# A planner that orders the instructions counts DMA loads as landing later, and four more weight buffers open once the weight conversion is over

## The chip, the cores and the metric

One core of one Trainium2 chip. The time is device microseconds (us) of one execution, taken from several runs; the profile is of one execution. Engines are named as in the profile: PE (TensorE matmul), PEld (TensorE weight load), DVE (VectorE), ACT (ScalarE), POOL (GpSimd), SP (SyncE, which here only issues DMAs; its queue is in order).

## The reference

Three layers follow one another on 4 batches of 448 tokens, 12 heads of 64:

```python
q_n, k_n = rmsnorm(q, g_q), rmsnorm(k, g_k)
scores = q_n @ k_n.T / sqrt(64); attn = softmax(scores)      # max subtracted, 1e-9 in the sum
x = (attn @ v), heads put side by side                       # 1792 x 768
x = max(x @ w_in, 0) ** 2 @ w_out                            # 768 -> 2048 -> 768
h = x @ w_in2; out = (max(h, 0) + alpha * min(h, 0)) @ w_out2
```

The inputs are float32. In the kernel the weights arrive as 64-bit words and are turned into float32 on the chip.

## The kernel before

**Arithmetic.** Each product of the two MLPs is made of three matmuls: every operand is split into a high part (`wh`) and a rest (`wl`), and high x rest, high x high and rest x high are added in PSUM. The weights are cut into units: 32 of the up projection (384 KB each, three 128-row blocks) and 24 of the down projection (512 KB, four blocks). A unit feeds 9 or 12 matmuls for one batch (`T = 1`), or 18 or 24 for two (`T = 2`).

**Three sources of a unit** (`weight`, L265). "first": the 64-bit words are loaded into a `raw` buffer (L282), ACT takes the absolute value of the high words into `ws` (L292), DVE does four steps on it (L294, L297, L301, L304), ACT copies the high part into a `whl` buffer (L251), POOL writes the rest (L259), and the finished pair is stored to DRAM (`w<-whl`, L311). "kept": the finished pair is loaded back from DRAM straight into a `whl` buffer (L279). "f64": like "first", without the store. There are three buffers each of `raw`, `ws` and `whl`, for the whole program.

**Stages.** `with_attention` (L422) holds the attention of all four batches, the first MLP of batch 0 (slot 0, units 0 to 55, source "first") and the first MLP of batch 1 (slot 1, units 56 to 111, source "kept"). The row maxima of the scores (L685 on PE, L689 on DVE) travel through PE and ACT into a small DMA (`mv<-mn`, L697) before the scores proper (L710) can start. `without` (L826) follows: the first MLP for batches 2 and 3 (units 112 to 167, "kept"), then the second MLP twice (units 168 to 279, "f64"), all with `T = 2`. The last lines of `with_attention` fetch units 112 to 114 ahead (L821 to L823).

**What sets the order.** The program is written out by a planner (`Tasks`, L53). Every step is a task with an urgency, the engines that may do it and a cost in us. The planner keeps a clock for each engine, always takes the task that can start first (of those within 0.05 us the one with the lower urgency number), and emits it. Every engine, and SP's queue with it, runs in the order of emission, so the costs decide only the order; the waits on the chip are real semaphores. A DMA of cost c that is issued at s is taken to land like this (L159 to L162):

```python
self.ends[e] = s + 0.06
self.dma = max(self.dma, s + 1.3) + t.on[e]
t.end = self.dma + 0.8
```

where the cost is the bytes over 350e3 (L210). By that account a 384 KB unit lands 3.22 us after its issue on an empty queue, a 512 KB unit after 3.60 us. Where several buffers of a pool are free, a task takes the one that came free first (`slot`, L179). MLP matmuls have the largest urgency numbers: PE does them when no attention step can start.

Of the kernel before, what the change touches and what calls it, by code (L numbers as in the profile page):

```python
# [26 lines left out]
UP, DN = 384, 512  # L27
# [25 lines left out]
class Tasks:  # L53
# [45 lines left out]
    def run(self):  # L99
        ready = {e: [] for e in self.ends}  # L100

        def offer(t):
            for e in t.on:
                ready[e].append(t)

        for t in self.new:
            for d in (*t.deps, *t.behind):
                if d.start is None:
                    t.missing += 1
                    d.next.append(t)  # L110
        for t in self.new:
            if not t.missing:
                offer(t)
        left = len(self.new)
        self.new = []
        while left:
            best = None
            for e, tasks in ready.items():
                found, soonest = [], None
                for t in tasks:  # L120
                    s = self.ends[e] + (max(t.gap, self.gap[e]) if e in "AV" else 0)
                    s = max(s, self.port) if e in t.alone else s
                    for d in t.deps:
                        s = max(s, d.end + (0 if d.engine == e == "T" else self.WAIT[e]))
                    for d in t.behind:
                        s = max(s, d.start)
                    taken = []
                    for b in t.bufs:
                        if b.ap is None:
                            taken.append(self.slot(b, taken))  # L130
                            s = max(s, taken[-1][0] + self.WAIT[e]) if taken[-1] else None
                            if s is None:
                                break
                    if s is None:
                        continue
                    if len(t.on) > 1:
                        other = min(max(self.ends[o], s, self.port if o in t.alone else 0) + self.PRICE[o] * t.on[o]
                                    + 0.7 * sum(x.on[o] for x in ready[o] if x.urgency < t.urgency)
                                    for o in t.on if o != e)
                        if s + self.PRICE[e] * t.on[e] > other + 0.2:  # L140
                            continue
                    found.append((s, t.urgency, t))
                    soonest = s if soonest is None else min(soonest, s)
                if found:
                    s, _, t = min((x for x in found if x[0] <= soonest + 0.05), key=lambda x: x[1])
                    if best is None or s < best[0]:
                        best = (s, e, t)
            assert best, "no task can start"
            s, e, t = best
            for o in t.on:  # L150
                ready[o].remove(t)
            for b in t.bufs:
                if b.ap is None:
                    _, n, b.pool = self.slot(b)
                    slots = self.free[b.pool]
                    b.slot = slots.pop(next(i for i, x in enumerate(slots) if x[1] == n))
                    b.ap = b.slot[2]
            t.engine, t.start = e, s
            if e == "S" and t.on[e]:  # L159
                self.ends[e] = s + 0.06  # L160
                self.dma = max(self.dma, s + 1.3) + t.on[e]
                t.end = self.dma + 0.8  # L162
            else:
                t.end = self.ends[e] = s + t.on[e]
                self.gap[e] = t.gap
                if e in t.alone:
                    self.port = t.end
            t.emit(e)
            left -= 1
            for b in t.bufs:  # L170
                b.left -= 1
                b.until = max(b.until, t.end)
                self.release(b)
            for n in t.next:
                n.missing -= 1
                if not n.missing:
                    offer(n)
# [29 lines left out]


def load(nbytes):
    return nbytes / 350e3  # L210


MM = 0.202
# [3 lines left out]
def attention_relu2_mlp_prelu_mlp(ctx: ExitStack, tc: tile.TileContext, qkt, qk_tm, v, gb, alpha, ident, sel,  # L217
# [10 lines left out]
    def pooled(pool, name, n, shape, dtype):  # L228
        ts.pool(name, [pool.tile(shape, dtype, name=f"{name}{i}") for i in range(n)])
# [6 lines left out]
    kept = {id(w1): [Buf(dram.tile([128, 2, UP], F32, name=f"w1_{i}")) for i in range(2 * KF)],  # L236
            id(w2): [Buf(dram.tile([128, 2, DN], F32, name=f"w2_{i}")) for i in range(4 * KD)]}
    y_dram = [[Buf(dram.tile([128, S], F32, name=f"y{b}_{d}")) for d in range(KD)] for b in range(2)]
    for name, n, dt, size in (("raw", 3, U32, 2 * DN), ("ws", 3, F32, DN), ("whl", 3, F32R, 2 * DN)):
        pooled(const, name, n, [128, size], dt)  # L240

    only = {}

# [21 lines left out]
    def weight(u, w, i, source, urgency, after):  # L265

        n = w.shape[-1] // 2
        both = Buf(pool="whl")
        parts = [(both, 0), (both, 1)]

        def part(k):
            return both.ap[:, k * n:k * n + n]

        def pair():
            return both.ap[:, :2 * n].bitcast(F32).rearrange("p (k n) -> p k n", k=2)

        if source == "kept":
            k = kept[id(w)][i]
            add(urgency, {"S": load(1024 * n)}, dma(pair, lambda: k.ap), [k], parts, "wh")  # L279
            return both  # L280
        raw, f = Buf(pool="raw"), Buf(pool="ws")
        add(urgency, {"S": load(1024 * n)}, dma(lambda: raw.ap[:, :2 * n], lambda: w[i]), [], [raw], "raw", after)  # L282

        def half(k):
            return raw.ap[:, :2 * n].rearrange("p (n two) -> p n two", two=2)[:, :, k]

        def fu():
            return f.ap[:, :n].bitcast(U32)


        add(urgency, {"A": act(n)},
            lambda e: nc.scalar.activation(out=f.ap[:, :n], in_=half(1).bitcast(F32), func=ACTF.Abs), [raw], [f], "f")  # L292
        add(urgency, {"V": dve2(n)},
            lambda e: nc.vector.tensor_scalar(out=f.ap[:, :n], in0=f.ap[:, :n], scalar1=TINY, scalar2=None, op0=ALU.max),  # L294
            [], [f])
        add(urgency, {"V": dve2(n)},
            lambda e: nc.vector.tensor_scalar(out=fu(), in0=fu(), scalar1=0x07FFFFFF, scalar2=3,  # L297
                                              op0=ALU.bitwise_and, op1=ALU.logical_shift_left), [], [f])

        add(urgency, {"V": dve(n)},  # L300
            lambda e: nc.vector.scalar_tensor_tensor(out=fu(), in0=half(1), scalar=0xC0000000, in1=fu(),  # L301
                                                     op0=ALU.bitwise_and, op1=ALU.bitwise_or), [raw], [f])
        add(urgency, {"V": dve(n)},
            lambda e: nc.vector.scalar_tensor_tensor(out=fu(), in0=half(0), scalar=29, in1=fu(),  # L304
                                                     op0=ALU.logical_shift_right, op1=ALU.bitwise_or), [raw], [f])
        add(urgency, on("wh", A=act(n), V=dve2(n)), lambda e: copy(e, part(0), f.ap[:, :n]), [f], [(both, 0)], "wh")
        add(urgency, on("wl", P=pool2(n), V=dve(n)), lambda e: rest(e, part(1), f.ap[:, :n], part(0)),
            [f, (both, 0)], [(both, 1)], "wl")
        if source == "first":
            k = kept[id(w)][i]  # L310
            add(urgency, {"S": load(1024 * n)}, dma(lambda: k.ap, pair), parts, [k], "keep")  # L311
        return both

    stream = []
    for s1, more in (("first", 0), ("kept", 0), ("kept", 2)):
        stream += [(w1, i, s1) for i in range(2 * KF)] + [(w2, i, s1) for i in range(4 * KD)]
        for _ in range(more):
            stream += [(w3, i, "f64") for i in range(2 * KF)] + [(w4, i, "f64") for i in range(4 * KD)]
    made, cur = {}, [0]

    def prepare(u, urgency, after=None):
        if u < len(stream) and u not in made:
# [99 lines left out]
    def with_attention():  # L422
        with ExitStack() as es:
# [378 lines left out]
            def give(bank):  # L802
# [3 lines left out]
                    ts.free["m"].append((bank.slot[0], bank.slot[1], bank.ap.rearrange("p (t n) -> p t n", t=1)))  # L806
                add(-100, {"S": 0}, emit, [], [bank], None, first_scores[0, H - 1])

            setup()
            attention(0, 0, True)  # L810
            for _ in range(2):
# [2 lines left out]
                prepare(u, 95, first_scores[0, 7])  # L814
            only.update(wl="P", wh="A")
            mlp(0, (0,), hg, to_dram(1, [y_dram[0]]), 10000, 140, 2.6)
            attention(1, 200)
            mlp(0, (1,), hg, to_dram(1, [y_dram[1]]), 20000, 340, 5.2)
            attention(2, 400)
            attention(3, 600)  # L820
            for u in range(cur[0], cur[0] + 3):  # L821
                prepare(u, 5000)
                made[u].open = True  # L823
            ts.run()

    def without():  # L826
        with ExitStack() as es:
            q1 = es.enter_context(tc.tile_pool(name="q1", bufs=1))
            pp = es.enter_context(tc.tile_pool(name="pp2", bufs=1, space=PSUM))
            hg = fixed(q1, [128, 2, KF, 2, S], F32R, "hg2")  # L830
            pooled(q1, "rl", 3, [128, 2, S], F32)
            pooled(q1, "y", 2, [128, 2, S], F32)
            pooled(pp, "m", 4, [128, 2, 512], F32)
# [83 lines left out]
```

## Time and profile before

| what | value |
|---|---|
| median of 3 runs | 1296.36 us (1292.48 to 1309.52) |
| profiled execution | 1297.45 us, its span 1295.6 us |
| PE busy | 1232.6 us (95%), 5790 matmuls |
| DVE, ACT, POOL busy | 800.8 (62%), 720.9 (56%), 373.5 us (29%) |
| mean granted TensorE clock | 0.978 of full |
| DMA | 194.45 MB, mean 150 GB/s |

The span is from the first to the last instruction; the 1.85 us around it are launch and end. Shares over the whole span mix two very different parts: `with_attention` ends and `without` begins at 590.9 us, and the profile has to be read on either side of that.

### The profile page before, as it was taken

The numbers are of one execution on the slowest core, as the hardware profiler recorded it, in microseconds if no ns is written. First come the engines' busy times: TensorE is split into PE (matmuls) and PEld (weight loads), VectorE is DVE, ScalarE is ACT, GpSimd is POOL, SyncE is SP. The second block draws the span as 40 slices with busy tenths as digits, with TensorE's granted clock in tenths as the row PEclk, the third lists the DMA queues.
The fourth block names the chain that finished last, engine by engine and source line by source line (L and its number), as shares of the span: only waits on it lengthen the run. The fifth ranks groups of instructions, "written<-read, shape, count | busy, mean of one in ns | idle before, by whom it ended". The sixth has DMA issues, their size and how long they took to land.

```text
span 1295.6 us, 16918 instructions
## 1 busy us (share of the span) xinstructions
PE 1232.6 (95%) x5790; PEld 1073.4 (83%) x5790; DVE 800.8 (62%) x1419; ACT 720.9 (56%) x1350; POOL 373.5 (29%) x354
## 2 busy tenths in 40 slices
PE   4997899797999899999999999999999999999998
PEld 2556677675888788888999999999999999999997
DVE  6688899999888688602111000487895548786550
ACT  4788689776699879823333000366653336664331
POOL 3245345535345525310000000222232222223221
PEclk7998999998999899999999999999999999999999
DMA  5136658788445544257333323233354333334330
GB/s 184 54 117 228 237 202 277 275 280 274 170 145 180 193 145 136 81 188 246 105 105 120 114 100 112 83 105 111 125 180 155 119 114 98 114 123 137 133 112 29
DMA packets 69014, 194.45 MB, mean 150 GB/s; under 512 B 8320, under 2 KB 14592, under 8 KB 68928
## 3 DMA queue, kind: packets, MB, share of 16 engines
q1 hardware_dynamic: 68928, 193.38, 45.1%
q8 instruction: 45, 0.74, 0.2%
q14 instruction: 41, 0.34, 0.1%
HBM read 159.84 MB, written 33.42 MB: 149 GB/s over the span
## 4 chain that ended last, share of the span: by engine, by line
PE 80%; DVE 10%; ACT 4%; DMA 3%; issue 2%; SPq 0%; POOL 0%; ACTq 0%; DVEq 0%
PE m L343 54%; PE bank L343 11%; PE bank L710 5%; PE pv L753 4%; PE pv L729 3%; PE bank L685 2%; DVE mc L689 1%; DVE ws L301 1%; DMA whl<-w 1%; DVE hl L259 1%; DVE ws L304 1%; DVE ws L294 1%; DMA tm<-in_qk_tm 1%; DMA raw<-in_w 1%; DVE ss L588 1%
## 5 line engine op out<-in xcount | busy, mean ns | idle before, releaser
L259 POOL TENSOR_TENSOR whl<-ws,whl 128x384 fp32r<-128x384 f32 (+2 forms) x169 | 204.9, 1215 | 683.4 <-ACT whl L251 405.2
L343 PE MATMUL m<-xs,whl 128*128 128x448 f32 x1728 | 350.8, 365 | 0.7 <-ACT rl L251 0.7
L343 PE MATMUL m<-hg,whl 128*128 128x448 f32 x1728 | 350.7, 365 | 0.0
L343 PEld LDWEIGHTS m<-xs,whl 128*128 128x128 f32 x1728 | 324.5, 188 | 26.7 <-ACT rl L251 1.1
L343 PEld LDWEIGHTS m<-hg,whl 128*128 128x128 f32 x1728 | 324.5, 188 | 25.7
L292 ACT ACTIVATE ws<-raw 128x384 f32<-128x384 f32 (+1 forms) x168 | 101.3, 603 | 133.5 <-POOL whl L259 112.3
L294 DVE TENSOR_SCALAR ws<-ws 128x384 f32<-128x384 f32 (+1 forms) x168 | 68.0, 409 | 142.6 <-ACT ws L292 142.4
L343 PE MATMUL bank<-xs,whl 128*128 128x448 f32 x576 | 142.4, 382 | 7.8 <-POOL xs L259 3.3
L251 ACT ACTIVATE whl<-ws 128x384 fp32r<-128x384 f32 (+1 forms) x167 | 94.4, 566 | 77.3 <-PE m L343 57.1
L343 PE MATMUL bank<-hg,whl 128*128 128x448 f32 x576 | 130.6, 369 | 2.2 <-DMA whl<-w 2.2
L343 PEld LDWEIGHTS bank<-xs,whl 128*128 128x128 f32 x576 | 111.5, 196 | 21.2 <-POOL xs L259 3.7
L343 PEld LDWEIGHTS bank<-hg,whl 128*128 128x128 f32 x576 | 108.9, 191 | 11.8 <-DMA whl<-w 2.6
L304 DVE SCALAR_TENSOR_TENSOR ws<-raw,ws 128x384 uint32<-128x384 uint32 (+1 forms) x168 | 116.3, 698 | 2.7
L689 DVE TENSOR_REDUCE mc<-bank 112x1 f32<-112x448 f32 x192 | 110.3, 615 | 11.4 <-PE bank L685 10.2
L259 DVE TENSOR_TENSOR hg<-m,hg 128x896 fp32r<-128x896 f32 x48 | 52.1, 1086 | 94.1 <-ACT hg L251 93.6
L301 DVE SCALAR_TENSOR_TENSOR ws<-raw,ws 128x384 uint32<-128x384 uint32 (+1 forms) x168 | 106.5, 639 | 3.7
L710 PE MATMUL bank<-mv,st 128*128 128x448 f32 (+2 forms) x352 | 102.2, 397 | 5.3 <-ACT mn L695 2.4
L259 DVE TENSOR_TENSOR hl<-bank,hl 128x448 fp32r<-128x448 f32 (+1 forms) x120 | 73.7, 618 | 32.6 <-ACT bank L718 31.5
L753 PE MATMUL pv<-hl,vhl 128*128 128x448 f32 x330 | 87.3, 374 | 1.3 <-DVE hl L259 1.3
L685 PE MATMUL bank<-st,mv 128*112 128x448 f32 x176 | 62.2, 411 | 22.5 <-DVE mc L689 7.8
L710 PEld LDWEIGHTS bank<-mv,st 128*128 128x128 f32 (+2 forms) x352 | 60.9, 182 | 24.9 <-DVE mc L689 6.3
L297 DVE TENSOR_SCALAR ws<-ws 128x384 uint32<-128x384 uint32 (+1 forms) x168 | 72.7, 439 | 3.6
(110 smaller groups left out, 1259.5 us busy)
## 6 DMA issues: line engine op xcount, KB each, us to landing
raw<-in_w SPq DMA_DIRECT2D x96, 384.0 KB
raw<-in_w SPq DMA_DIRECT2D x72, 512.0 KB
whl<-w SPq DMA_DIRECT2D x64, 384.0 KB
whl<-w SPq DMA_DIRECT2D x48, 512.0 KB
w<-whl SPq DMA_DIRECT2D x32, 384.0 KB
w<-whl SPq DMA_DIRECT2D x24, 512.0 KB
qk<-in_qkt SPq DMA_DIRECT2D x24, 448.0 KB
tm<-in_qk_tm SPq DMA_DIRECT2D x40, 224.0 KB
```

The source lines that it names most:

```text
L251: nc.scalar.activation(out=o, in_=i, func=ACTF.Copy)
L259: (nc.gpsimd if e == "P" else nc.vector).tensor_tensor(out=o, in0=x, in1=hi, op=ALU.subtract)
L292: lambda e: nc.scalar.activation(out=f.ap[:, :n], in_=half(1).bitcast(F32), func=ACTF.Abs), [raw], [f], "f")
L294: lambda e: nc.vector.tensor_scalar(out=f.ap[:, :n], in0=f.ap[:, :n], scalar1=TINY, scalar2=None, op0=ALU.max),
L297: lambda e: nc.vector.tensor_scalar(out=fu(), in0=fu(), scalar1=0x07FFFFFF, scalar2=3, op0=ALU.bitwise_and, op1=ALU.logical_shift_left), [ ...
L301: lambda e: nc.vector.scalar_tensor_tensor(out=fu(), in0=half(1), scalar=0xC0000000, in1=fu(), op0=ALU.bitwise_and, op1=ALU.bitwise_or), [ ...
L304: lambda e: nc.vector.scalar_tensor_tensor(out=fu(), in0=half(0), scalar=29, in1=fu(), op0=ALU.logical_shift_right, op1=ALU.bitwise_or), [ ...
L343: nc.tensor.matmul(out=acc.ap[:, t, :S], lhsT=w.ap[:, part * n + 128 * kk:part * n + 128 * kk + 128], rhs=src(h, k0 + kk, t)[1](), start=( ...
L685: lambda e, t=t, pm=pm: nc.tensor.matmul(out=pm.ap[:CP, :S], lhsT=m.ap[:, 0, t * CP:(t + 1) * CP], rhs=s.ap[:, 0, :], start=True, stop=Tru ...
L689: lambda e, t=t, pm=pm: nc.vector.reduce_max(out=mc.ap[:, t:t + 1], in_=pm.ap[:CP, :S], axis=AX.X),
L710: nc.tensor.matmul(out=pa.ap[:keys, :S], lhsT=s.ap[:rows, k, c:c + keys], rhs=m.ap[:rows, k, :], start=(k == 0), stop=(k == 1))
L753: nc.tensor.matmul(out=o.ap[:, :S], lhsT=l, rhs=r, start=(n == 0 and x == 0), stop=(half and x == 1))
```

## The change

Three constants of the planner's account of a DMA become larger: 1.3 to 2.0, 0.8 to 1.4, and the rate 350e3 to 320e3. By the new account a 384 KB unit lands 4.63 us after its issue, a 512 KB unit after 5.04 us, and the small `mv<-mn` after 3.45 instead of 2.15 us. No DMA is added or removed by that; only the order of emission can differ.

The `raw` and `ws` buffers are no longer allocated for the whole program. `with_attention` has its own set, which is closed once the last step of unit 55 has been emitted (`no_more`); in its place (18 KB of each partition) four more buffers of the size of `whl` are opened (16 KB), and the loads of units 56 to 111 may land in any of the seven. Units 112 to 114 use the three `whl` buffers alone, as everything in `without` does. `without` allocates a new set of `raw` and `ws`, in space that `with_attention` used.

```diff
-                self.dma = max(self.dma, s + 1.3) + t.on[e]
-                t.end = self.dma + 0.8
+                self.dma = max(self.dma, s + 2.0) + t.on[e]
+                t.end = self.dma + 1.4
...
 def load(nbytes):
-    return nbytes / 350e3
+    return nbytes / 320e3
...
-    for name, n, dt, size in (("raw", 3, U32, 2 * DN), ("ws", 3, F32, DN), ("whl", 3, F32R, 2 * DN)):
-        pooled(const, name, n, [128, size], dt)
+    pooled(const, "whl", 3, [128, 2 * DN], F32R)
+
+    def converting(pool):
+
+        pooled(pool, "raw", 3, [128, 2 * DN], U32)
+        pooled(pool, "ws", 3, [128, DN], F32)
...
-        both = Buf(pool="whl")
+        both = Buf(pool=("whl", "more") if "more" in ts.free else "whl")
...
-        add(urgency, on("wl", P=pool2(n), V=dve(n)), lambda e: rest(e, part(1), f.ap[:, :n], part(0)),
+        converted[0] = add(urgency, on("wl", P=pool2(n), V=dve(n)), lambda e: rest(e, part(1), f.ap[:, :n], part(0)),
...
+            wp = es.enter_context(ExitStack())
+            converting(wp.enter_context(tc.tile_pool(name="wp", bufs=1)))
+
+            def no_more():
+
+                def emit(e):
+                    until = max(x[0] for n in ("raw", "ws") for x in ts.free[n])
+                    wp.close()
+                    pool = wp.enter_context(tc.tile_pool(name="wq", bufs=1))
+                    ts.free["more"] += [(until, i, pool.tile([128, 2 * DN], F32R, name=f"more{i}")) for i in range(4)]
+
+                add(-100, {"S": 0}, emit, [], [], None, converted[0])
+
+            ts.pool("more", [])
...
             mlp(0, (0,), hg, to_dram(1, [y_dram[0]]), 10000, 140, 2.6)
+            no_more()
             attention(1, 200)
...
+            del ts.free["more"]
             for u in range(cur[0], cur[0] + 3):
                 prepare(u, 5000)
                 made[u].open = True
+            ts.pool("more", [])
             ts.run()
+            del ts.free["more"]
...
             hg = fixed(q1, [128, 2, KF, 2, S], F32R, "hg2")
+            converting(q1)
```

## Rows read from the trace of the kernel before

**Rows 1.** Busy by stretch: PE, PEld, DVE, ACT, POOL us (count), clock, DMA share, GB/s.

```profile
98.00:343.00 245.00, 212.34 (x920) 169.72 (x919) 226.54 (x442) 188.53 (x391) 110.33 (x96) 0.94 0.72 248
343.00:440.00 97.00, 95.73 (x465) 82.13 (x464) 78.00 (x139) 87.38 (x189) 48.42 (x51) 1.00 0.51 162
440.00:555.00 115.00, 111.64 (x538) 97.43 (x537) 84.14 (x148) 94.27 (x202) 43.09 (x44) 0.97 0.40 131
555.00:590.90 35.90, 33.01 (x164) 30.00 (x163) 1.24 (x2) 5.32 (x10) 3.46 (x3) 1.00 0.61 202
590.90:1291.60 700.70, 700.65 (x3456) 648.99 (x3456) 340.02 (x552) 273.78 (x415) 130.47 (x112) 1.00 0.36 119
```

**Rows 2.** PE's waits, 343 to 591 us: total us, times, longest.

```profile
PE bank L343 <- DMA whl<-w: 5.5, 2, 3.3
```

**Rows 3.** The chain of waits, 343 to 591 us: start us, us, what.

```profile
438.81 6.90 DMA whl<-w
...
568.48 6.96 DMA whl<-w
```

**Rows 4.** Busy by stretch, PE alone: us, busy (count), clock, DMA share, GB/s.

```profile
310.00:320.00 10.00, 3.40 (x9) 0.57 0.63 191
...
400.00:440.00 40.00, 39.82 (x196) 1.00 0.57 180
440.00:450.00 10.00, 6.74 (x24) 0.73 0.72 248
450.00:460.00 10.00, 10.00 (x49) 0.93 0.49 156
```

**Rows 5.** PE's waits, 98 to 343 us.

```profile
PE bank L685 <- DVE mc L689: 7.8, 5, 2.9
PE bank L685 <- ACT ws L292: 6.2, 1, 6.2
```

**Rows 6.** Timeline from 310.79 us: start us, us, engine, line, operation.

```profile
310.79 0.69 DVE L304 SCALAR_TENSOR_TENSOR ws<-raw,ws 128x512 uint32<-128x512 uint32 x1
...
315.02 1.28 DVE L304 SCALAR_TENSOR_TENSOR ws<-raw,ws 128x512 uint32<-128x512 uint32 x2
...
316.76 1.14 DVE L689 TENSOR_REDUCE mc<-bank 112x1 f32<-112x448 f32 x2
...
317.51 0.69 PE L685 MATMUL bank<-st,mv 128*112 128x448 f32 x1 [6.24 <-ACT ws L292]
```

**Rows 7.** The chain of waits, 98 to 343 us, shares of it by line.

```profile
by line: PE bank L343 15.3%; issue 8.8%; DVE ws L301 6.8%; PE pv L729 6.3%; DVE ws L304 5.6%; DVE hl L259 4.8%; DVE ws L294 4.8%; PE bank L710 4.4%; DMA raw<-in_w 3.8%; DVE mc L689 3.6%; PE bank L685 3.5%; DVE ws L297 3.0%; ACT ws L292 2.5%
```

**Rows 8.** Timeline from 590 us: loads issued on SP, and ACT that waits for them.

```profile
590.01 0.32 SPq L262 DMA_DIRECT2D whl<-w  x1
...
591.21 1.47 SPq L262 DMA_DIRECT2D raw<-in_w  x3
...
594.81 0.33 SPq L262 DMA_DIRECT2D whl<-w  x1
595.62 0.55 ACT L292 ACTIVATE ws<-raw 128x384 f32<-128x384 f32 x1 [4.80 <-DMA raw<-in_w]
...
596.74 0.55 ACT L292 ACTIVATE ws<-raw 128x384 f32<-128x384 f32 x1 [0.57 <-DMA raw<-in_w]
...
597.70 0.56 ACT L292 ACTIVATE ws<-raw 128x384 f32<-128x384 f32 x1 [0.41 <-DMA raw<-in_w]
```

**Rows 9.** Timeline of SP from 343 us, where the loads of kept parts begin.

```profile
343.16 0.32 SPq L262 DMA_DIRECT2D whl<-w  x1
...
344.05 0.58 SPq L262 DMA_DIRECT2D mv<-mn  x1
```

**Rows 10.** Costliest groups of the page: busy, mean ns, idle before.

```profile
L259 POOL TENSOR_TENSOR whl<-ws,whl 128x384 fp32r<-128x384 f32 (+2 forms) x169 | 204.9, 1215 | 683.4 <-ACT whl L251 405.2
```

**Rows 11.** PE's waits over the whole span: the start's.

```profile
PE bank L636 <- DVE rhl L551: 7.3, 1, 7.3
```

More of the change, by code (lines that the diff above doesn't have):

```diff
@@ L318, in attention_relu2_mlp_prelu_mlp @@
             stream += [(w3, i, "f64") for i in range(2 * KF)] + [(w4, i, "f64") for i in range(4 * KD)]
-    made, cur = {}, [0]
+    made, cur, converted = {}, [0], [None]
     def prepare(u, urgency, after=None):
```

## The prediction

> **What bounds the kernel now.** I read the busy time by stretch first [rows 1], because the 95% of PE is an average over two programs. From 590.9 us on PE is busy 700.65 of 700.70 us with 3456 matmuls, 4.93 a us at full clock: that is `without`, it is bound by matmuls, and nothing that only moves loads can shorten it. All that can be won lies before. From 98 to 343 us, where attention shares the engines with the conversion of units 0 to 55, PE is busy 212.34 of 245 us, DVE 226.54 (92%), and the clock is 0.94 of full: DVE is what is short. From 343 us the parts are kept ones, DVE falls to 80% and then 73%, and PE is busy 95.73 of 97 and 111.64 of 115 us; the last 35.9 us before 590.9 hold almost only MLP matmuls (DVE 1.24 us), and PE idles 2.89 of them.
>
> Second, who ended PE's waits. After 343 us it is a kept load, 5.5 us in two waits [rows 2], and the chain of waits shows where: a load issued at 438.81 let PE go 6.90 us later, another at 568.48 after 6.96 us [rows 3]. In the first part it is DVE: the row maxima (7.8 us in five waits), and one wait of 6.2 us that the view puts down to ACT [rows 5]. The timeline says what that one is [rows 6]: from 310.79 to 316.30 us DVE does conversion steps without a break, the row maxima of L689 stand behind them until 316.76, and PE starts again at 317.51. The chain there has the raw loads at 3.8% of 245 us, 9.3 us, against 20.2% for the four conversion steps on DVE [rows 7]: loads are a small part of that stretch.
>
> **The change, part by part.**
>
> *Four more buffers for kept parts.* A kept load can be issued when a buffer comes free, so with three buffers a unit is under way while PE uses the two before it; at 4.93 matmuls a us and 9 a unit that covers 2 x 1.83 = 3.7 us, at 12 a unit 4.9 us. The two loads in the chain took 6.9 us, so PE had to stop. With seven buffers six units cover 11.0 us at least, more than the longest landing seen: both stops go. Their price is more than the idle time, since the clock falls to 0.73 and 0.93 in the stretches after the first [rows 4]. I count matmuls: 24 + 49 = 73 from 440 to 460 us, where 400 to 440 us has 4.9 a us, 98 in 20 us; 25 are missing, 5.1 us. From 555 to 590.9 us there are 164 where 4.93 a us makes 177: 2.7 us, with the short stop at the turn to `without` in it. Sum **-7.8 us**; the bounds are the idle time alone, 3.3 + 2.9 = 6.2 us, and, with the whole clock loss added (0.27 x 10 + 0.07 x 10 = 3.4), 9.6 us. It lies wholly on PE's path, as PE is the only engine near full there. After it nothing is late: what PE does next on that stretch is matmul after matmul.
>
> *What these buffers cost.* `no_more` emits no instruction. The first loads into the new space wait on SP for the last POOL and DVE readers of `raw` and `ws`; behind them in SP's queue stands a `mv<-mn` that the scores need (now issued 0.9 us after the first kept load [rows 9]). One POOL step is 1.2 us [rows 10], so 0 to 1.2 us. Then four extra loads of 384 KB go out close together; at 1.04 us for each further 384 KB (the mean step between the landings of [rows 8]) they take 4.2 us, which one such small DMA may stand behind: 0 to 4.2 us, once. I take 0, as PE has MLP matmuls to do meanwhile and idles 1.27 us in all from 343 to 440 us [rows 1]; without that cover it is up to 5.4 us.
>
> *New `raw` and `ws` in `without`.* They lie in space that attention and slot 1 used, so the first three raw loads wait for the last matmul of slot 1, and kept loads stand behind them on SP. Now they are issued at 591.21 us, just after that matmul anyway, and the next kept load at 594.81 [rows 8]. Three units are ready by then; at 18 matmuls each they last 54 / 4.93 = 11 us, to 602 us, and the kept load, landing some 4.4 us after issue, is there at 599.2: 2.7 us of slack. Cost 0.
>
> *Later loads in the planner's account.* Nothing is issued more or less; what can move is the order on SP, PE, ACT, DVE and POOL from 0 to 590.9 us. Which account is nearer? Three raw loads go out at 591.21 us behind a kept load of 590.01, and ACT, idle and waiting, gets them at 595.62, 596.74 and 597.70 [rows 8]: 4.4 us to the first, 1.0 to 1.1 us for each further 384 KB. The old account says 3.22 and 1.12 us, the new one 4.63 and 1.23. So on a queue in use the new one is within 0.3 us, the old one 1.2 us short. The Trainium skill has a rule that speaks against the change: its page "DMA: Bandwidth & Descriptors", section on the anatomy of one DMA, fits a DMA (measured on the GpSimd queue) as 2.0 us plus the bytes at 436 GB/s, which would be an estimated 2.9 us for 384 KB. By it the new account would hold every load back 1.7 us too long and this term would be a loss of the third rival's size, and the sum its 1305 us. That rule is not what the row shows: 4.4 us, and the term is taken by the row.
>
> What is a better account worth from 98 to 343 us? There PE lacks what DVE hasn't done yet. The upper end of a gain: half of PE's idle time, 32.66 / 2 = 16 us, if bursts like [rows 6] dissolve. The end on the other side: the stretch 310 to 320 us has 9 matmuls where 49 fit [rows 4], 8.2 us lost to one burst; four more of them are 33 us. I take **0**: DVE's sum of work in that stretch is not changed, it has only 18.5 us idle, and the raw loads are 9.3 us of its chain, most of it beside DVE work. Up to 98 us the longest wait is the start's 7.3 us for the first norms [rows 11]; the loads there shift alike in the account, `mv<-mn` by 1.3 us, for which none of PE's waits is put down to it now: 0, with half that wait, 4 us, as the end on either side.
>
> Sum: 1297.45 - 7.8 = 1289.7 us for the profiled execution; the median of the runs is 1.1 us lower, so 1288.6, rounded to **1289 us**.
>
> **The rivals.**
>
> *The better account also pays before 343 us.* For: raw loads hold 9.3 us of the chain [rows 7], and six conversion steps ahead of a row maximum [rows 6] are what an order made with wrong times could look like. Against: DVE at 92%. Half the idle time of PE on top: 1289 - 16 = 1273 us.
>
> *No change.* The buffers do not do what they say: the stops at 445 and 575 us are not for want of buffers but of transfer rate, and seven loads in the queue only land later each. For: DMA moved 248 GB/s from 440 to 450 us [rows 4]. Against: alone, MLP matmuls want 384 KB in 1.83 us or 512 KB in 2.43 us, some 215 GB/s, and a 384 KB load has landed 1.04 us after the one before it [rows 8], which is 378 GB/s. Then 1296 us, the median.
>
> *Slower.* In slot 0 there are still three `whl` buffers, and by the new account each is held 1.4 us longer by the store that empties it: about 6.3 us instead of 4.9 for a 384 KB unit (ACT 0.42, POOL 0.96, waits 0.3, store 4.63, all the planner's costs). A planner that sees fewer weights ready lets PE's filler matmuls stand later and bunches conversion on DVE, so that more row maxima stand behind bursts. Against: 56 units in 245 us are 4.4 us a unit, while three buffers held 6.3 us each give one in 2.1 us; it decides only where the planner's own DMA queue is full as well (DMA is busy 0.72 on average). Two more bursts of 8.2 us give 1289 + 16 = 1305 us; from five more on, 1330 us, it is slower by over 2%.
>
> **How the numbers follow.** Chances: the forecast 0.55 (its own range 1282 to 1295), no change 0.13, the gain before 343 us 0.15, slower 0.17. The range 1272 to 1304 holds the first two, two thirds of the third and some of the fourth: a little over 8 in 10. Over 2%, about what a measurement of this kernel can tell from no change, means under 1270 or over 1322 us. Below lies a third of the third case, 0.05; above a third of the last, 0.06; within, 0.89.
>
> **What would show it.** PE's waits after 343 us without a kept load over 1 us, about 98 matmuls from 440 to 460 us, and `without` starting at 583 us instead of 590.9 with its 700.7 us unchanged, would show the first term right. If the stretch from 98 us to the first kept load is still about 245 us with DVE over 90% busy, the second term's 0 is right; if it is longer by a burst or two with waits for L689, the third rival is. The forecast is wrong if `without` has waits of PE, or if the start moves by over 4 us.

## The result, and the profile after

The kernel after takes 1281.02 us (median of 4 runs, 1279.44 to 1283.90) against 1294.43 us (median of 4 runs, 1292.48 to 1309.52); the ratio is 0.9912, 95% interval 0.9887 to 0.9937. A second measurement beside its parts, below, gave 0.9929 (0.9908 to 0.9951). So it is faster by 0.7 to 0.9%, 10 to 13 us, within the 2% that was forecast as likeliest and 8 us under the 1289 us of the forecast, 1 us below the range of 1282 to 1295 us that was its own.

The busy time by stretch of the kernel after (us busy and count for PE, PEld, DVE, ACT, POOL; clock, DMA share, GB/s), for the stretches of [rows 1], the last two cut where the second program starts now:

```profile
98.00:343.00 245.00, 216.58 (x948) 173.92 (x947) 231.42 (x448) 195.57 (x408) 118.24 (x96) 0.95 0.76 255
343.00:440.00 97.00, 96.87 (x478) 85.34 (x477) 77.78 (x138) 90.30 (x193) 50.47 (x51) 1.00 0.61 193
440.00:555.00 115.00, 114.92 (x571) 102.00 (x570) 80.16 (x142) 91.18 (x194) 42.24 (x43) 1.00 0.45 140
555.00:572.50 17.50, 16.82 (x83) 15.15 (x81) 0.00 (x0) 1.09 (x2) 0.00 (x0) 1.00 0.36 110
572.50:1273.50 701.00, 700.87 (x3456) 649.63 (x3456) 340.14 (x552) 273.19 (x414) 129.85 (x112) 1.00 0.38 119
```

The second program starts at 572.5 us instead of 590.9 and takes the same 701 us. From 343 us to there PE is idle 0.9 us; before it was 7.5 us, and its clock is 1.00 throughout. From 98 to 343 us it does 948 matmuls where it did 920: something was won there too. PE's waits from 343 us to the second program are one, and the stretch of [rows 4] around the old stop is full:

```profile
PE m L347 <- ACT rl L255: 0.7, 1, 0.7
```

```profile
440.00:460.00 20.00, 20.00 (x104) 1.00 0.60 199
```

Nothing waits for a kept load any more [rows 2, 3]; 104 matmuls stand in the 20 us that had 73. From 98 to 343 us PE's two longest waits, in all, times, longest, against [rows 5]:

```profile
PE bank L347 <- POOL xs L263: 5.2, 1, 5.2
PE bank L689 <- DVE mc L693: 4.7, 4, 2.6
```

The wait of 6.2 us behind the burst of [rows 6] is gone, others have come. The opening of the new buffers on SP's queue:

```profile
339.83 2.22 SPq L266 DMA_DIRECT2D more<-w  x4
```

The four loads leave within 2.22 us, and SP is not held by the readers of `raw` and `ws`.

**A measure for the parts.** One stretch of time holds different work in two orders. So I cut each profile where PE has done a given amount of matmul work: each matmul counted at 0.2028 us (700.7 us over the 3456 of the second program), those of L529 and L729 (lines of the kernel before) at 0.75 and 0.405, the small transposes at 0.07. The work of 70 us is done near 98 us (attention of batch 0 over), that of 250 us near 325, that of 340 us near 420. The stretches are of the one profiled execution of each kernel, the median is of all its runs. The table stands for all runs below; times in us.

| kernel | account | more buffers | work 70 to 250 | 250 to 340 | 340 to 2nd program | 2nd program | median, before beside it |
|---|---|---|---|---|---|---|---|
| before | old | 0 | 229.1 | 95.0 | 169.3 | 700.7 | 1294.4 |
| before again | old | 0 | 228.2 | 95.0 | 166.8 | 700.7 | one run 1294.6, 1292.8 |
| account only | new | 0 | 224.7 | 93.7 | 165.1 | 700.7 | 1287.3, 1293.3 |
| buffers only | old | 4 | 225.9 | 95.4 | 162.9 | 702.7 | 1292.3, 1293.3 |
| one more | new | 1 | 226.9 | 93.6 | 161.6 | 700.7 | 1283.7, 1293.3 |
| after | new | 4 | 223.3 | 93.5 | 159.9 | 701.1 | 1281.0, 1294.4 |
| after again | new | 4 | 224.1 | 93.5 | 160.0 | 700.7 | 1283.1, 1293.3 |
| old, then new | both | 4 | 228.2 | 96.7 | 159.3 | 701.5 | 1288.0, 1292.8 |
| new, then old | both | 4 | 224.2 | 93.6 | 162.3 | (718.0) | 1287.9, 1292.8 |
| later still | 6.06 us | 4 | 237.7 | 97.0 | 160.6 | 701.1 | 1302.3, 1292.8 |
| midway | 3.92 us | 4 | 223.5 | 97.9 | 161.4 | (714.9) | 1287.4, 1292.6 |
| small DMA old | new but one | 4 | 228.2 | 93.2 | 161.1 | 700.7 | 1287.0, 1292.6 |
| small DMA new | old but one | 4 | 229.2 | 95.8 | 161.9 | 702.1 | 1294.3, 1293.3 |
| matmul 0.203 | new | 4 | 225.4 | 94.0 | 160.2 | 701.0 | 1284.5, 1293.3 |

The two numbers in brackets are of executions in which every matmul of the second program was 2% slower (last section), and say nothing of their kernels.

### The profile page after: what moved, and what is told of

Read it like the earlier page. It is cut to its first block, busy times and chain, and to the rows that moved or that the text cites. A ratio compares the mean times of both kernels' runs of the same rounds, so it can differ in the third digit from the quotient of the medians.

```text
span 1277.7 us, 16933 instructions
## 1 busy us (share of the span) xinstructions
PE 1225.7 (96%) x5790; PEld 1072.1 (84%) x5790; DVE 797.4 (62%) x1414; ACT 720.9 (56%) x1353; POOL 382.8 (30%) x356
## 4 chain that ended last, share of the span: by engine, by line
PE 80%; DVE 10%; ACT 4%; issue 2%; DMA 2%; POOL 1%; SPq 0%; ACTq 0%; DVEq 0%; POOLq 0%
PE m L347 54%; PE bank L347 12%; PE bank L714 5%; PE pv L757 4%; PE bank L689 2%; PE pv L733 2%; DVE mc L693 2%; DVE ws L305 1%; DVE ws L308 1%; DMA tm<-in_qk_tm 1%; DVE bank L645 1%; DVE ws L298 1%; DVE st L263 1%; DVE ss L592 1%; DVE mv L263 1%
## 5 line engine op out<-in xcount | busy, mean ns | idle before, releaser
L308 DVE SCALAR_TENSOR_TENSOR ws<-raw,ws 128x384 uint32<-128x384 uint32 (+1 forms) x168 | 120.1, 717 | 2.7
L305 DVE SCALAR_TENSOR_TENSOR ws<-raw,ws 128x384 uint32<-128x384 uint32 (+1 forms) x168 | 106.6, 637 | 3.8
L347 PE MATMUL bank<-xs,whl 128*128 128x448 f32 x405 | 99.7, 381 | 7.0 <-POOL xs L263 5.2
L347 PE MATMUL bank<-hg,whl 128*128 128x448 f32 x420 | 97.9, 375 | 3.6 <-ACT whl L255 2.6
L714 PE MATMUL bank<-mv,st 128*128 128x448 f32 (+2 forms) x352 | 98.0, 387 | 1.1 <-DVE hl L263 0.6
L347 PEld LDWEIGHTS bank<-xs,whl 128*128 128x128 f32 x405 | 77.6, 194 | 17.3 <-POOL xs L263 5.5
L347 PEld LDWEIGHTS bank<-hg,whl 128*128 128x128 f32 x420 | 81.0, 195 | 12.0 <-ACT whl L255 3.4
```

Source lines behind the costliest of these rows:

```text
L347: nc.tensor.matmul(out=acc.ap[:, t, :S], lhsT=w.ap[:, part * n + 128 * kk:part * n + 128 * kk + 128], rhs=src(h, k0 + kk, t)[1](), start=( ...
L714: nc.tensor.matmul(out=pa.ap[:keys, :S], lhsT=s.ap[:rows, k, c:c + keys], rhs=m.ap[:rows, k, :], start=(k == 0), stop=(k == 1))
```

## The experiments

Theory 1: each part has its own gain, the account before 343 us and the buffers after it. Theory 2: the account does it all. Theory 3: the buffers do it all.

**The account alone.**

In the kernel before:

```diff
-                self.dma = max(self.dma, s + 1.3) + t.on[e]
-                t.end = self.dma + 0.8
+                self.dma = max(self.dma, s + 2.0) + t.on[e]
+                t.end = self.dma + 1.4
...
-    return nbytes / 350e3
+    return nbytes / 320e3
```

> The kernel before with the three constants of the new account and nothing else (three buffers for kept parts throughout). If the two parts of the change each have their own gain (theory 1: the account re-orders the stretch before 343 us, the buffers end the stops on kept loads after it), the time to the first kept load is some 3 to 9 us shorter than before, the stops on kept loads stay (5 us of waits in the rest), and the time is 1286 to 1291 us against 1294.4. If the account does it all (theory 2: told that loads land late, the planner sets MLP matmuls later, and three buffers do), it is 1281 us without waits on kept loads. If the buffers do it all and the shorter first part of the profile is scatter (theory 3), it is 1292 to 1297 us.

Measured: 1287.27 us, ratio 0.9956 (0.9935 to 0.9978). In the profile it is 5 us shorter from the work of 70 us to that of 340 us, as theory 1 has it. But it is also 3 us shorter after it (against the mean of the two profiles of before), with three buffers. PE's waits on kept loads there:

```profile
PE bank L343 <- DMA whl<-w: 2.3, 3, 1.5
```

Less than half of the 5.5 us of [rows 2], in three small pieces. What changed near the first stop is the order of the loads. SP's queue in the kernel before, and at the same place here:

```profile
437.08 1.39 SPq L262 DMA_DIRECT2D qk<-in_qkt  x2
438.81 0.33 SPq L262 DMA_DIRECT2D whl<-w  x1
```

```profile
436.68 0.33 SPq L262 DMA_DIRECT2D qk<-in_qkt  x1
437.11 0.61 SPq L262 DMA_DIRECT2D whl<-w  x1
...
438.27 0.39 SPq L262 DMA_DIRECT2D qk<-in_qkt  x1
```

In the kernel before, the load that PE stopped for (issued at 438.81 us, let go 6.90 us later [rows 3]) stands right behind two loads of `qk`, 448 KB each; here a kept load stands between the two, and PE's wait for it is 1.5 us, the longest of the three. No run changes that order alone. It is not that PE comes to the units later: from the issue of a kept load to the first matmul of its unit it is 8.7 us on average here, against 8.9 and 8.8 us in the two profiles of before. Neither theory 1 nor theory 2 is right as it stood.

**The buffers alone.**

In the kernel after, as in all that follow:

```diff
-                self.dma = max(self.dma, s + 2.0) + t.on[e]
-                t.end = self.dma + 1.4
+                self.dma = max(self.dma, s + 1.3) + t.on[e]
+                t.end = self.dma + 0.8
...
-    return nbytes / 320e3
+    return nbytes / 350e3
```

> The kernel after with the three constants of the old account (four more buffers, new raw and ws in the second program). Theory 1: up to 343 us the same order as before, so the same time to within 1 us; after it no wait on a kept load and 4.9 matmuls a us; 1294.4 - 9.5 = 1285 us. Theory 2: waits on kept loads stay at 4 us or more, 1290 us or more. Theory 3: 1281 us.

Measured: 1292.28 us, ratio 1.0008 (0.9980 to 1.0036). No gain that can be told: theory 3 falls, and so does my 1285 us. Until the kept loads begin, near 340 us, the order of instructions on every engine is that of the kernel before, as expected, but the time is not the same to within 1 us: 225.9 us from the work of 70 us to that of 250, against 229.1 and 228.2. No wait on a kept load is left while slot 1 runs, and that stretch is 5 us shorter than the mean of the two profiles of before (which are of executions 3.0 and 1.8 us above the medians in the table). But some of it is given back at the turn to the second program. The timeline there, PE and SP:

```profile
582.93 14.92 PE L347 MATMUL m<-xs,whl 128*128 128x448 f32 x72 [0.68 <-ACT rl L255]
599.57 4.73 PE L347 MATMUL m<-xs,whl 128*128 128x448 f32 x22 [1.71 <-DMA whl<-w]
```

```profile
585.82 1.29 SPq L266 DMA_DIRECT2D raw<-in_w  x3
...
587.63 1.23 SPq L266 DMA_DIRECT2D whl<-w  x1
593.33 0.33 SPq L266 DMA_DIRECT2D raw<-in_w  x1
...
594.66 0.43 SPq L266 DMA_DIRECT2D whl<-w  x1
```

The new `raw` buffers are issued 2.9 us after the second program's first matmul (before, 0.3 us after [rows 8]), and the kept loads stand behind them in SP's queue. That alone does not stop PE: the kernel after has the same delay, raw loads at 575.50 us after a start at 572.5, and no wait. There both kept loads go out next:

```profile
577.30 3.12 SPq L266 DMA_DIRECT2D whl<-w  x2
```

By the old account a fourth raw load and two loads of `y` stand between the two, and the second kept load leaves 11.7 us after the start instead of 7.6. It is that one which PE runs dry for, after 72 matmuls, for 1.7 us.

**One more buffer instead of four.**

```diff
-...for i in range(4)]
+...for i in range(1)]
```

> The kernel after with one more buffer in place of four. With four buffers three units cover 5.5 us (up projection) or 7.3 us (down projection), against the 6.9 us that two loads took: theory 1 expects at most 2 us of waits on kept loads, in the up projection, and 1281 to 1285 us. If seven buffers were needed, waits on kept loads come to 3 us or more and the time to 1286 us or more. Theory 2: 1281 us, as the number of buffers does not matter.

Measured: 1283.74 us, ratio 0.9935 (0.9912 to 0.9959), no wait on a kept load, 161.6 us for the kept stretch. A single buffer gives most of what four give (160.0 us). That is more than the bare cover said: three units of the up projection last 5.5 us, less than the 6.9 us of the slow landings, and yet PE never waited for a kept load.

**The kernel after again, and before again** (no edit).

> The kernel after once more, on the same chip as its parts, so that the parts can be set against it: 1281 us in every theory, without waits on kept loads. The scatter of the profiled stretches before 343 us against the first profile of this kernel says what a difference of a few us there is worth: under 1.5 us if the order alone sets it.

> The kernel before once more, for a second profile of it, as the profiled execution was 3 us above the median of its runs. If the stops on kept loads near 445 and 575 us belong to the order of this kernel, they are here again (4 us or more of waits on kept loads after 343 us) and the rest from matmul work done at 325 us to the second program is 264 us, within 1.5. If they were this one execution's, waits on kept loads are under 3 us and that rest is some 260 us.

After again: 1283.05 us, and 224.1, 93.5 and 160.0 us in the table's stretches, within 0.8 us of the first profile; only the first 45 us differ, by 2.7 us. Before again: one stop on a kept load instead of two, and 261.8 us from the work of 250 us to the second program instead of 264.3:

```profile
PE bank L343 <- DMA whl<-w: 3.0, 1, 3.0
```

So the stop near 445 us belongs to the kernel's order, the second one (2.2 us) to that execution. The first profile overstates what the three buffers cost by up to 2.5 us.

What one order is worth in different executions can be read further. Until the kept loads begin, near 340 us, the traces have the same order of instructions on every engine in before, before again, buffers only and "old, then new" (the old account), and likewise in account only, one more, after, after again and "new, then old" (the new one). From the work of 70 us to that of 250 the first four take 225.9 to 229.1 us, the other five 223.3 to 226.9: 3 to 4 us of scatter within one order, and means of 227.9 and 224.6, 3.2 us apart.

**Each account in its own stretch.** The account becomes a variable that is switched where the four buffers open; it begins as (1.3, 0.8, 32 / 35), and in the reverse the two are exchanged.

```diff
-                self.dma = max(self.dma, s + 2.0) + t.on[e]
-                t.end = self.dma + 1.4
+                until, after, rate = self.account
+                self.dma = max(self.dma, s + until) + t.on[e] * rate
+                t.end = self.dma + after
...
+                    ts.account = (2.0, 1.4, 1.0)
                     wp.close()
```

> The kernel after, but planned by the old account up to the point where the four buffers open and by the new one from there. If the account earns its gain in both stretches (3.4 us before 343 us and 4.8 us after it, read from the four profiles with either account), this has the second alone: 1286 to 1287 us against 1283 for the kernel after. If its gain lies all in the first stretch, 1290 us or more; if all in the second, 1283 us.

> The kernel after, but planned by the new account up to the point where the four buffers open and by the old one from there. Gain in both stretches: 1287 to 1288 us. All in the first stretch: 1283 us. All in the second: 1290 us or more. In each case no stop on a kept load over 1 us while slot 1 runs, as seven buffers cover the landing in either account.

Measured: 1288.02 us (ratio 0.9959, 0.9940 to 0.9979) and 1287.88 us (0.9955, 0.9938 to 0.9973). Both lie about midway between buffers only and the kernel after: the account earns some 4 to 5 us on either side of 343 us. In the second stretch that is the kept stretch itself (162.3 and 162.9 us by the old account, 159.3 to 160.2 by the new one) and the wait at the turn, 1.7 and 2.0 us with the old account (0.5 us in "old, then new", none in the kernel after). The change also moves the buffers to other places in memory; the first stretch goes with the account and not with the place, 224.7 us with the new account in the old places (account only) and 228.2 us with the old account in the new ones ("old, then new").

**Later still.**

```diff
-                self.dma = max(self.dma, s + 2.0) + t.on[e]
-                t.end = self.dma + 1.4
+                self.dma = max(self.dma, s + 2.7) + t.on[e]
+                t.end = self.dma + 2.0
...
-    return nbytes / 320e3
+    return nbytes / 290e3
```

> The kernel after with loads counted later still (2.7 and 2.0 us, 290e3: 6.06 us for a 384 KB unit). If the account helps because it comes near the real landing (4.4 us on a queue in use), one that is 1.6 us beyond it helps no more: 1283 to 1289 us. If later is simply better (the planner keeps more work ahead of each load), it is 1278 to 1281 us.

Measured: 1302.25 us, ratio 1.0068 (1.0045 to 1.0091): slower than the kernel before, and more than was expected for it. The loss is all in the conversion stretch. Its busy time from 98 to 343 us, and PE's longest wait there in the timeline, with what DVE did before it:

```profile
98.00:343.00 245.00, 207.54 (x879) 164.40 (x880) 230.21 (x433) 186.31 (x394) 114.97 (x98) 0.92 0.67 229
```

```profile
122.31 1.16 PE L689 MATMUL bank<-st,mv 128*112 128x448 f32 x2 [11.99 <-DVE st L263]
```

```profile
116.90 0.98 DVE L298 TENSOR_SCALAR ws<-ws 128x384 f32<-128x384 f32 x2
...
121.54 0.63 DVE L263 TENSOR_TENSOR st<-bank,st 64x448 fp32r<-64x448 f32 x1
```

From 116.90 to 121.51 us nine conversion steps stand on DVE right ahead of the `st` step that PE waits for; in the 6.6 us before them DVE does mostly attention steps. Over the whole stretch DVE is as busy as ever, but with more attention: from 98 to 343 us it does 192 conversion steps where the kernel after does 216, PE gets 480 MLP matmuls where it gets 561 (both counted in the trace, the latter in the second profile of after), and the first of them starts at 105.9 us instead of 98.5. PE has fewer matmuls to fill its waits with. That is the third rival, at a landing of 6.06 us instead of 4.63.

**Midway.**

```diff
-                self.dma = max(self.dma, s + 2.0) + t.on[e]
-                t.end = self.dma + 1.4
+                self.dma = max(self.dma, s + 1.65) + t.on[e]
+                t.end = self.dma + 1.1
...
-    return nbytes / 320e3
+    return nbytes / 335e3
```

> The kernel after with an account halfway between old and new (1.65 and 1.1 us, 335e3: 3.92 us for a 384 KB unit). If the time follows the account smoothly (old with seven buffers 1292, new 1283, later still 1302), this lies between 1283 and 1292 us, near 1287. If each account only deals a new order with its own luck, it can be anywhere from 1279 to 1302 us, outside of 1283 to 1292 as likely as in it.

Measured: median 1287.42 us against 1292.64; the ratio is 0.9984 with an interval of 0.9958 to 1.0010, as three of its twelve executions lie at 1298 to 1301 us. The profile is of one of these three; before its second program the matmuls that follow each other directly come at the usual pace, 201 ns apart from 230 to 340 us as in the kernel after. The median is where a smooth curve would have it, but the stretches are not: 223.5 us as in the kernel after, then 97.9, the worst of all. ACT's waits for raw loads from 98 to 343 us do go smoothly with the account, 9.5 us in the kernel before, 3.6 here and 0.6 in the kernel after.

**The small DMA apart.** The DMA of the row maxima alone keeps the old constants, and in the reverse alone has the new ones.

```diff
-                self.dma = max(self.dma, s + 2.0) + t.on[e]
-                t.end = self.dma + 1.4
+                small = t.on[e] == 0.05
+                self.dma = max(self.dma, s + (1.3 if small else 2.0)) + t.on[e]
+                t.end = self.dma + (0.8 if small else 1.4)
```

> The kernel after with the small DMA of the row maxima (mv, 1.8 KB) counted by the old constants and all loads and stores of weights, inputs and results by the new ones. If the gain before 343 us comes from the loads and stores of weights counted later, it stays: 1282 to 1284 us, and 224 us from the attention of batch 0 to 325 us. If it comes from the scores being planned 1.3 us later behind that DMA, it goes: 1286 us or more, and 228 us.

> The reverse of the run before: only the small DMA of the row maxima is counted by the new constants, all other loads and stores by the old ones (four more buffers). If the 4 us before 325 us hang on the scores being planned later behind that DMA, they are here: 224 us for that stretch, and with the kept stretch of the old account (256 to 258 us) 1287 to 1289 us. If the order of each account is a throw of its own, that stretch is anywhere from 223 to 229 us; 228 us and 1291 us or more would say that the small DMA alone does nothing.

Measured: 1287.01 us (ratio 0.9961, 0.9941 to 0.9981) and 1294.32 us (1.0041, 1.0011 to 1.0072). With the small DMA counted early the first stretch is back at 228.2 us, as expected if it carries that gain; but counted late alone it gives nothing, 229.2 us (four of the twelve executions of this kernel lie at 1305 to 1309 us, which widens its ratio). By these two profiles and medians the gain of the first stretch needs both, though each is one order with the scatter of 3 to 4 us that executions have. The first of these kernels has ACT's waits for raw loads at 0.6 us like the kernel after, and its conversion steps on DVE in 91 runs between 98 and 343 us (before 62, after 82, counted in the trace), so shorter bursts on average. Neither is therefore what pays by itself. What it has instead is a wait for row maxima of 6.1 us:

```profile
PE bank L690 <- DVE mc L694: 9.3, 5, 6.1
```

**A nudge that has nothing to do with DMAs.**

```diff
-MM = 0.202
+MM = 0.203
```

> The kernel after with a planner's cost that has nothing to do with DMAs moved by half a per cent: a matmul counted 0.203 instead of 0.202 us. The order of emission differs from early in the second attention on. If the account is what pays, the time stays within 2 us of the kernel after: 1281 to 1285 us, 223 to 226 us for the stretch before 325 us. If such a nudge alone moves the time by 4 us or more, differences of that size between the accounts are the luck of an order, and only the larger ones (the account later still, 19 us) are shown.

Measured: 1284.45 us, ratio 0.9929 (0.9912 to 0.9945); 225.4 and 94.0 us. That is 1.4 us above the kernel after beside its parts (1283.05), whose own two medians lie 2.0 us apart: this nudge cannot be told from scatter. From the work of 70 to that of 340 us the five profiles by the old account take 321.3 to 325.0 us ("small DMA new" and "old, then new" among them), the six by the new one 316.8 to 320.5 ("new, then old" and the nudge, at 319.4, among them): the two do not overlap, and their means differ by 5 us, where executions of one order differ by up to 3.7. But one nudge is one draw, and "midway" and "small DMA old" are orders by accounts between the old and the new one that lie 4 us above it.

## Why the prediction came out as it did

- **What bounds the kernel.** Right: the second program kept its 701 us (700.7 to 702.7) in all profiles but the two in brackets, and nearly everything came from before it.
- **Four more buffers, -7.8 us.** The mechanism is shown: with two units of cover PE stops at a landing of 6.9 us, and with one more buffer, by the same account, the stops go (1287.27 to 1283.74 us). The 6.9 us are not what a kept load takes in general: others were used as early as 4.3 us after their issue without a wait, and the one of 438.81 us stood behind two `qk` loads. The stretch from the work of 340 us on went from 168.1 (mean of two) to 159.9 us, -8.1. That this is so near -7.8 is partly luck. The step that failed is the attribution: I gave all of it to the buffers, and counted 2.7 us for a second stop that another execution of the same kernel does not have. By themselves the buffers bring -5.2 us there and lose 2.0 in the second program, whose one wait of 1.7 us is at the turn; the account by itself brings -3.0 us with three buffers, where the order of the loads near the first stop is another. By the medians beside 1293.26 us the account alone is worth 6.0 us, the buffers alone 1.0 and both 10.2, so 3.2 us are there only with both. I had costed the later account for 0 to 590.9 us as a whole by looking only at the stretch before 343. By my own sign `without` would start at 583 us; it started at 572.5.
- **What the buffers cost, 0.** Right: four loads in 2.22 us, PE without a wait from 343 to 440 us.
- **New `raw` and `ws`, 0.** Right for the kernel after, but on a thinner margin than I said. I took the raw loads to leave as soon as the last matmul of slot 1 is over; they left 3.0 us after the second program's start, with the kept loads behind them, and by the old account, which lets a fourth raw load go ahead of the second kept load, PE waits 1.2 to 2.0 us (the three kernels with four more buffers whose loads are counted by it).
- **Later loads in the account, 0 before 343 us.** Wrong, and this is the term that was mis-sized: 3.2 us up to the work of 250 us (means of four and five profiles of one order each) and 1.5 from there to 340, and some 4 to 5 us by the medians of "old, then new" and "new, then old". The argument was that DVE's sum of work is fixed and DVE is 92% busy. It is, and DVE's busy share rose to 94% (231.42 of 245 us): the 18.5 us that it idled were not as fixed as I took them. This is the first rival, at less than a third of its price of 16 us.
- **No change, the second rival.** Not so: from 440 to 460 us the DMAs moved 199 GB/s in the kernel after and 202 before (the mean of 248 and 156 [rows 4]), and PE had no stop there, so the rate of transfer was not what stopped it.
- **Slower, the third rival.** Its mechanism is real and stood one step further on: not at 4.63 us but at 6.06, where PE lacked filler matmuls and the time was 1302 us. I had put it at bunching of conversion on DVE. The longest wait does end behind such a bunch, nine steps, but over the stretch conversion fell behind attention.
- **The rule on a DMA's time.** By the Trainium skill's fit (page "DMA: Bandwidth & Descriptors", the anatomy of one DMA; made on the GpSimd queue) a 384 KB load takes an estimated 2.9 us, and the old account of 3.22 would have been the nearer one. The measurement decides: accounts of 3.22, 3.92, 4.63 and 6.06 us gave 1292, 1287, 1281 to 1283 and 1302 us with seven buffers, and the best of them is next to the 4.4 us of [rows 8], a load with one kept load ahead of it.

What stays open is what in the order before 343 us pays. Shorter bursts and fewer waits of ACT for raw loads go with the gain, but "small DMA old" has both without it; and with so few orders tried, the part of the 5 us that is better knowledge and the part that is a lucky order cannot be parted by these runs. Open too is what makes the kept stretch with seven buffers some 3 us shorter by the new account: no wait on a kept load is left there by either. Shown is that the account is worth 4 to 5 us on either side of 343 us, and that the loss at 6.06 us is far outside the scatter.

## What to carry to other kernels

A planner's latency of loads changes the whole order, that of the loads in their queue included, so it acts on waits that look as if only a buffer could end them: here on the stop near 445 us and on the wait at the turn. Set it by landings in the trace on a queue in use, and try one step beyond, where lack of filler shows. Before costing a buffer, count the units in flight against the longest landing, and look at what stands ahead of that load in the queue: here one buffer more did nearly all that four did. When an order is rewritten, profile the same order more than once and nudge an unrelated cost several times, to know what scatter and a new order alone are worth before reading a few us as a cause.

## What the runs showed of the hardware

The same 3456 matmuls came at two rates with the granted clock recorded as 1.00. Busy time from 700 to 800 us, in the second program, of "midway" and then of after again:

```profile
700.00:800.00 100.00, 100.00 (x486) 90.83 (x485) 5.71 (x9) 7.49 (x13) 0.00 (x0) 1.00 0.32 106
```

```profile
700.00:800.00 100.00, 100.00 (x495) 92.66 (x495) 5.78 (x10) 5.42 (x11) 0.07 (x1) 1.00 0.32 108
```

486 matmuls in 100 us, 206 ns each, against 495, 202 ns, for the whole of the second program (714.9 and 700.7 us); "new, then old" had it too (718.0 us). PE waited for nothing in either. What sets the rate was not tried. The first 45 us of one program also differed by 2.7 us between two executions (after and after again), 2.0 of them by 17 us.
